# First chunk's turned blocks in the transform's input tiles, u turned ahead of them, next z loaded a chunk earlier, and a new instruction order

## The chip, the core and the metric

The kernel runs on one core of a Trainium2 chip. The metric is the device time of one execution in microseconds (us), lower is better. The engines are TensorE (PE, matmuls; PEld is its weight load), VectorE (DVE), ScalarE (ACT), GpSimd (POOL) and SyncE (SP, which here only issues DMAs). Each engine runs its own instructions strictly in the order in which they were written; they meet through semaphores.

## The reference

Eight batches of a gated attention unit, followed by a long-convolution block. All of it is one launch.

```python
# u, v: (8, 3136, 256)   z: (8, 3136, 64)
attn = maximum((z @ z.T) / S, 0) ** 2          # S = 3136, per batch
x    = u * (attn @ v)                          # (8, 3136, 256)
x1, x2, x3 = split(x @ w_proj, 3)              # 256 -> 3 x 256
conv = irfft(rfft(x2, axis=seq) * rfft(filter, axis=seq))
out  = (x1 * conv * x3) @ w_out
```

## The kernel before

**Tiling.** The sequence of 3136 is cut into 25 row tiles of 128 and, as columns, into seven chunks of 512, 512, 512, 512, 512, 256 and 320. Work goes batch by batch and chunk by chunk. For a chunk, a *unit* is a pair of row tiles: PE multiplies z with z into a PSUM pair `ps_s` (score, two 64-row matmuls side by side in the array), ACT or DVE applies the relu into an f32 tile `R_t` (L1899 on ACT, L1901 on DVE), ACT or DVE squares it into a bf16 tile `A_t` (L1908, L1910), and PE weighs v with it into two PSUM accumulators `ps_o` (L556, or L1701 when the rows are split in two halves). When all units of a chunk are weighed, DVE multiplies by u, which lies transposed in `uT_t`, and writes `xT_t` (L1954). The projection, the gates and a DFT of the middle part follow; after the seventh chunk of a batch its spectrum is multiplied by the filter's (`xh`) and transformed back, and `yT_t`, the output matmul and the store end the batch. This transform runs beside the next batch's chunks.

**Symmetry.** The score matrix is symmetric. Where a unit's row tiles belong to one of the next two chunks (REACH = 2), its squared tile is also turned by a DMA transpose from SP (function `mirror`, L1829) into a tile M1 or M2 (`M_t`, `M2e_t`, `M2o_t`), and the later chunk weighs that instead of computing it again. The squared tile must stay until the turn has landed. Squared tiles come from a pool of eight, used in a ring (`A_p`). In the first chunk of the first batch four of thirteen units are turned: two into M1 for chunk 1, two into M2e for chunk 2.

**Loads.** u is loaded and cast to bf16 by POOL's DMA into `un_t` (L630) and turned by SP into `uT_t` (`load_uT`, L1513). v is loaded by POOL (L649). The next batch's z comes in four pieces of 8, 8, 6 and 3 row tiles (`casts_at`): POOL loads a piece into `zn_t` (L630), DVE doubles it into `zd_t` (L1550), SP turns it into `zT_t` (L1557). Each chunk's loads are released on POOL by a copy of one element of the chunk's `xT_t` (`tick`, L639). The four pieces are released by the chunks 1 to 4 of the batch before.

**Order.** Nothing is scheduled at run time. A planner in the kernel's Python walks all tasks with a table of costs and writes the instructions out. The kinds of PE's tasks follow a fixed string ORDER, one letter a task: S score, W weigh, w and v the two halves of a row-split weighing, Q the spectrum's matmuls on quarters of the array, A, B and Z other matmuls. A second string, ENGINES, says for each task that ACT or DVE could do which of them does it. The order on DVE, ACT, SP and POOL comes out of the planner's own estimate of when a task is ready: for a DMA this is the end of its issue, its share of a common bus (`plan.bus`), a fixed time and an extra `late=` given with the task. These numbers decide only the order; at run time each instruction waits on semaphores.

```python
if task.moves:
    self.bus = max(end + DMA_GO[engine], self.bus) + task.moves
    lat = self.bus + DMA_DONE + task.late - end
```

Other pools that the change touches are `conv_in` (`c_p`, two tiles of 128 x 1024) and `spec_in` (`l_p`, two of 128 x 2048). They hold the inputs of the transform, which first needs them after the first chunks of the first batch.

Of the kernel before, what the change touches and what calls it, by code (L numbers as in the profile page):

```python
# [41 lines left out]


ORDER = (
    "ASBSWASWSWASWwSASvWSwSSWvwSSvSWSwSvSWWWWSSWWWWSSWWWWWSwSvSAWSAAAWAWAWWWBWSSWWAWWSAWWBSSAWWBSSwSvwSvA"
    "AwSWSvSWWWBBWWWABWAWSSAWBWAAWAWSSWSAWWBWWWWWSWSSWWBWSSSWWWWBWWAAWASwSAABWWWSSSvWWASSWAWWWWAAWWBAWAAA"
    "WAWSwSSvWWSSSWWWAAWWBAWASSWAABWAWWAWBwSSwSWAvSSvSWWWWWAWWSSWAAWWAWWSSWSSSWWAWSwSvQQwWSSWAAWvSQSWWAAW"
    "WSQAAWWAAWWQwwASSvSwwSAWAAWQvSSAWSvQvSWWWSQSWWWAAWWWAWSwSSWAWAvQwSwQvSwvSSvSWWAAWWAAWWWSQQWWWAAWSSSW"
    "WWAWQwQQvwQSSvAWASAWWWWAAWWASSWAWAAWWQSSWSSAWWSQQWAWWQSSWAWWAQQWWWWQSAWWAWWAWWSwSAvwSQvSWAWWASSWWAWW"
    "SSSWWWASSWAAWwSSvwSWWSwvSvSWWWWSSWWWWAWAWBABWSwSvSSWBWSSwSvWABWBWASSBWWAWBWBWSAWWAABWSSAAWAAWAWAWBAA"  # L50
    "SAWBASSWSSWBBAWWSSAWBWWBBBWWWWABWSSSWWSSAWAWWSQSWQAWAWWSSAWWWBAWBAWWWBQSAWWQwSwwSSWAAAWBWBAQvQvvSSQW"
    "BWSQQWWWBAWAWBAWWABWQSAWWASQWQSAWSSwwSvSvSWWWAAWWSQQWWWWWAASWWAWWSSAWQSSWWAAWAWQSWWAWSSWWAWWwSSvSWWS"
    "SSWWAWAWSSWAWWWWSSAWAWBWWASSWBWBBWSSSWWAABWSSSWWABWABWWSSSWWAWBBWAWAWWBASSWSSWAAAWBWSABWBBSwSvSWASWW"
    "BWBAWSWWABWWWSSSWwSSvAWBBWAAAWSSABWAAWBQQWAAWSSQWWWAWABWWQWSSWAWWQQSWBWWSSQWBWQSSWAAAWWAWWBWWSQSWWAA"
    "WWSSQWWSQSWWWQSQWAWAWSSWWAWWWWAABWAQSWAWWWABwSSAWAWWSQSvWWQSSWWAAWWASAWSSAWWSSSWWWSSSWWAWWAWAWWWWSSS"
    "WWWBBWAWSSSwwwSSvSvWWBvSSBBWBWAWWAAASWBBWBWAAWWBWASSAAWWBBSSWWWSSABWBSSwWASvSBWABWBBWSAWWBWWWBASSWAA"
    "SSAWABWSSWAAWABSQWAAWBBWQSSWWAWWSSQWWAAWWSQAWWWAWWWQQSWWWQSSWWBWQSSWAAAWWWSSQWWAWAWQSWAAWWASQWSQwSWA"
    "WAWAASSvBAWSWAWWBWWQQSWWWWWAAWSSQWWAAWAWWSQSWWAWAWWWSSSWAAWAWSSSwwwSvSvWWWSSvAAWWAWWWWSSSWWWBBBWBSSA"
    "WBABWSSSWBABSWABWSSWAWBAWWBSBWAAAWSSWWWBWBSSWAWASSWBBAWWSwSSvSWAWWBWWSSSWWWBAWWAWBAWSSBWWAAAWWSSQWAB"
    "AWWWSQSWWAAWAWAWBWAWSSAWAWSSSWWAASwQvSQWWSQSWWWAAAWSABBWWAWWQQSWWWSQwQWvSSWBWAAAWWSSSWWWWAQQWWWSQQWW"  # L60
    "WBAWAWSQBWAWSQSWWAAAWWASSWWWSSQWWWAWWSSWWSwSSvSwWWWWASvSAWWWAWAAWWSSAAWWSSWBWSSSWBWABAWSSSWABWBABWWW"
    "ASSWABWAABWWABWAWSSSWWBAWSSSWWBBWBABWBAWSSAABWBBWWAAWWWSSSWWBWBWSSWAAWSSAAWSSwQwSWAAWWBBQSvSvSWWWWAB"
    "WAWSQQWWAWABWQQSWWBWWSSSWAWWWQSSWWAAAWWWSSSWWAAASQAAWWQSAWAAWSQQWAAAWWQSQWWWAWWBWWSQSWWWWAWAQSwWWQvS"
    "SWAAAWSWWWSAWWSSAAAWWWwSSvSWAASSWWSSSWWWABWWWBSSBWWAWBBSBAWWBWAWBWSSSWWBSSWWABSSWBABWWWSSSWWWWBBWWBW"
    "WSSSWBAWwSSAAWBWBASAWWSvSSWWWASSWAWBBWWWZAAWWSSSWWABBWSQSWWWQSSWBBWWWWQQSWWWWAAWWAQSWAWSQQWWSSSWWWSS"
    "QWWWWBWBWWSQSWAAWWSSWWQSQWWWQSSWWWQSQWWWBWAWAWBAWWSSWAWAWSSAAWWQSSWWAWWAWWWQSZWWWSSSWWAWSSSWWWAWWWWW"
    "WWZZAAZBAAZZBBZZBBZBBZZZBZZQQZQZQZBQZQQQBZBQQQQZQQQQBZZZZZZZBZZZZBZZZZBBZZZBBBBBBBBBBBBBBBBBBBBBBBBB"
    "BBB"
)
# [357 lines left out]
def kernel(  # L427
# [1374 lines left out]
    def mirror(un, q_):  # L1802
# [12 lines left out]
                runs.append((a, i, [t]))  # L1815
        for a, i, ts in runs:
            made = mirror_tasks.setdefault((b, c, a), [])
            rows = N1 if ts[-1] == NT - 1 else P

            def go(a=a, i=i, ts=ts, rows=rows):  # L1820
                if (b, c, a) not in mirrors:
                    mirrors[b, c, a] = m_pool(c, a).tile()
# [6 lines left out]
                nc.sync.dma_start_transpose(out=o, in_=live[un][:rows, ds(i * cw, len(ts) * cw)])  # L1829
# [218 lines left out]
```

## Time and profile before

| | us |
|---|---|
| median of 3 runs (lowest, highest) | 977.6 (975.66, 978.12) |
| the profiled execution | 977.31 |
| its span, first to last instruction | 975.5 |
| PE busy | 950.4 (97%) |
| DVE busy | 870.8 (89%) |
| ACT busy | 836.0 (86%) |
| POOL busy | 197.4 (20%) |

Matmuls are pipelined, so that their durations overlap: what one costs is the distance from start to start. The end of the bracket in a row of the time line is how long the engine was idle before the instruction, and on what. A row of SP gives the time that the queue spent on issuing, not the landing; the landing is seen where somebody waited for it.

### The profile page before, as it was taken

Reading aid. Unit: us, or ns where it says so; the run is one execution under the profiler, and the core shown is the slowest. Engines: PE = TensorE matmul, PEld = TensorE weight load, DVE = VectorE, ACT = ScalarE, POOL = GpSimd, SP = SyncE. Lnnn points to the kernel's source line nnn. Section 1 sums busy time; section 2 is a strip of 40 time slices with the busy share of each in tenths; the row PEclk is TensorE's granted clock in tenths of the full one; section 3 lists DMA queues with packets and bytes.
Section 4 is the critical chain, followed back from the end, with each engine's and each line's share of the span. In section 5 each row is a group of like instructions: output and inputs, shape, how many; then the busy total and the mean of one; then the engine's idle time right before and its main releaser. Section 6 shows DMA issues by size and latency. Waiting matters only on the chain.

```text
span 975.5 us, 20058 instructions
## 1 busy us (share of the span) xinstructions
PE 950.4 (97%) x7097; PEld 469.8 (48%) x7097; DVE 870.8 (89%) x1508; ACT 836.0 (86%) x1145; POOL 197.4 (20%) x426
## 2 busy tenths in 40 slices
PE   6899999999999999999999999999999999999996
PEld 2344644445444554445544465444554455444654
DVE  7897998999889888899988999899899988889896
ACT  7686799999889998988898989799978899899783
POOL 5133311132012211213111131113201311000031
PEclk9999999999999999999999999999999999999998
DMA  9989889979799998988899999997999979786668
GB/s 151 148 161 171 135 171 165 172 142 167 168 199 202 135 177 188 199 172 134 178 200 192 169 154 179 216 184 143 152 201 210 187 139 182 179 190 142 179 195 259
DMA packets 332406, 170.36 MB, mean 175 GB/s; under 512 B 242598, under 2 KB 307942, under 8 KB 332304
## 3 DMA queue, kind: packets, MB, share of 16 engines
q1 hardware_dynamic: 302496, 132.43, 64.4%
q0 software_dynamic: 29168, 35.13, 24.5%
q10 hardware_dynamic: 640, 1.51, 0.5%
q8 instruction: 56, 0.92, 0.4%
q14 instruction: 46, 0.38, 0.1%
HBM read 90.26 MB, written 53.35 MB: 147 GB/s over the span
## 4 chain that ended last, share of the span: by engine, by line
PE 85%; DVE 6%; DMA 5%; issue 1%; ACT 1%; SPq 1%; POOL 0%; ACTq 0%; DVEq 0%; POOLq 0%
PE ps_o_t L556 45%; PE ps_s L556 35%; PE ps_o_t L1701 5%; DMA zn_t<-in_z_dram 1%; DVE A_t L1910 1%; DMA conv_in_t<-spec 1%; DVE R_t L1901 1%; DMA gs_t<-spec 1%; DMA spec_in_t<-spec 1%; DVE yT_t L1401 1%; DVE xh L1304 0%; DVE xT_t L1954 0%; DMA uT_t<-un_t 0%; DVE gate_t L1212 0%; DMA spec<-s_t 0%
## 5 line engine op out<-in xcount | busy, mean ns | idle before, releaser
L556 PE MATMUL ps_o_t<-A_t,v_t 128*128 128x512 bf16 (+2 forms) x1832 | 420.6, 356 | 3.8 <-DVE xT_t L1954 1.9
L1899 ACT ACTIVATE R_t<-ps_s 128x1024 f32<-128x1024 f32 (+2 forms) x351 | 328.3, 967 | 56.7 <-PE ps_s L556 51.8
L556 PEld LDWEIGHTS <-v_t 128*128 128x128 bf16 x2462 | 221.7, 98 | 231.6 <-issue 68.6
L1908 ACT ACTIVATE A_t<-R_t 128x1024 bf16<-128x1024 f32 (+3 forms) x310 | 301.8, 991 | 17.7 <-DVE R_t L1901 12.8
L1910 DVE TENSOR_TENSOR A_t<-R_t 128x1024 bf16<-128x1024 f32 (+3 forms) x186 | 207.5, 1128 | 10.1 <-ACT R_t L1899 7.1
L1901 DVE TENSOR_SCALAR R_t<-ps_s 128x1024 f32<-128x1024 f32 (+3 forms) x161 | 176.9, 1108 | 22.9 <-PE ps_s L556 17.4
L556 PE MATMUL ps_s<-zT_t 64*128 64x512 bf16 (+5 forms) x1355 | 165.0, 356 | 2.9 <-DVE R_t L1901 1.4
L639 POOL COPY tick<-xT_t 1x1 bf16<-1x1 bf16 x54 | 10.6, 196 | 692.0 <-DVE xT_t L1954 673.5
L556 PE MATMUL ps_s<-xT_t,wp 128*128 128x512 bf16 (+2 forms) x422 | 110.4, 353 | 0.3 <-DVE R_t L1901 0.3
L556 PEld LDWEIGHTS <-zT_t 64*128 64x128 bf16 (+1 forms) x1388 | 51.6, 99 | 90.8 <-issue 70.6
L589 ACT ACTIVATE x_t<-ps_s 128x512 bf16<-128x512 f32 (+2 forms) x133 | 72.8, 567 | 19.9 <-PE ps_s L556 16.8
L1954 DVE SCALAR_TENSOR_TENSOR xT_t<-ps_o_t,uT_t 128x256 bf16<-128x256 f32 (+2 forms) x224 | 75.9, 381 | 13.4 <-PE ps_o_t L556 8.2
L1304 DVE TENSOR_TENSOR xh<-xh,H 128x1024 bf16<-128x1024 bf16 x120 | 82.1, 685 | 2.9 <-ACT xh L589 1.1
L1212 DVE TENSOR_TENSOR gate_t<-ps_s,x_t 128x256 bf16<-128x256 f32 (+2 forms) x210 | 71.3, 383 | 9.3 <-PE ps_s L556 4.8
L556 PE MATMUL ps_o_t<-M_t,v_t 128*128 128x512 bf16 (+2 forms) x320 | 73.5, 353 | 0.0
L1401 DVE TENSOR_TENSOR yT_t<-ps_s,gate_t 128x512 bf16<-128x512 f32 (+2 forms) x96 | 58.3, 620 | 5.5 <-PE ps_s L556 4.6
L630 POOL DMA_DIRECT2D un_t<-in_u_dram x112 | 59.9, 556 | 7.4 <-issue 6.6
L649 POOL DMA_DIRECT2D v_t<-in_v_dram x112 | 59.6, 557 | 5.4 <-issue 3.5
L556 PEld LDWEIGHTS <-wp 128*128 128x128 bf16 x448 | 40.9, 98 | 39.7 <-issue 10.2
L556 PE MATMUL ps_s<-wp,xT_t 128*128 128x256 bf16 x398 | 58.6, 273 | 0.0
L1701 PE MATMUL ps_o_t<-A_t,v_t 64*64 64x512 bf16 (+4 forms) x562 | 56.7, 350 | 0.0
L556 PE MATMUL ps_s<-wo,yT_t 128*128 128x256 bf16 (+1 forms) x360 | 54.8, 273 | 1.1 <-DVE yT_t L1401 0.8
(170 smaller groups left out, 984.5 us busy)
## 6 DMA issues: line engine op xcount, KB each, us to landing
out_dram<-ost_t SPq DMA_DIRECT2D x60, 256.0 KB
spec<-s_t SPq DMA_DIRECT2D x96, 128.0 KB
spec_in_t<-spec SPq DMA_DIRECT2D x56, 192.0 KB
spec<-gs_t SPq DMA_DIRECT2D x56, 192.0 KB
v_t<-in_v_dram POOLq DMA_DIRECT2D x80, 128.0 KB, 4.6
un_t<-in_u_dram POOLq DMA_DIRECT2D x80, 128.0 KB, 5.5
conv_in_t<-spec SPq DMA_DIRECT2D x34, 256.0 KB
out_dram<-ost_t SPq DMA_DIRECT2D x18, 128.0 KB
```

Of the source, the lines that this page charges most:

```text
L556: wrote(nc.tensor.matmul(o, *args, **kw), o)
L589: got = nc.scalar.activation(out_, in_, AF.Copy)
L630: nc.gpsimd.dma_start(out=t[ds(j * N1, N1), lo - t0 : hi - t0, :], in_=x[:, n2 : n2 + hi - lo, :])
L1212: got = nc.vector.tensor_tensor(g[:, ::-1] if h == 0 else g, p, x, ALU.mult)
L1304: nc.vector.tensor_tensor(x[:, 1 - i], x[:, 0], h, ALU.mult)
L1401: got = nc.vector.tensor_tensor(yb["y"][:, dh, 0:w], p, gates[b, c, dh][:, 0:w], ALU.mult)
L1701: row_sums[dh] = h, nc.tensor.matmul(*args, **kw)
L1899: has_read(nc.scalar.activation(r, p, AF.Relu), p)
L1901: has_read(nc.vector.tensor_single_scalar(r, p, 0.0, ALU.max), p)
L1908: nc.scalar.activation(a, r, AF.Square)
L1910: (nc.vector if e == "DVE" else nc.gpsimd).tensor_tensor(a, r, r, ALU.mult)
L1954: nc.vector.scalar_tensor_tensor(x, f, inv_s2, ut, ALU.mult, ALU.mult)
```

## The change

The four turned units of the first chunk get their squared tiles from `conv_in` and `spec_in` in turn (`sends`), not from the ring. Of the first chunk's turns, the third and the fourth are issued only after u's first transpose has been issued. The pieces of the next z are released by chunks 0 to 3 from the second batch on; in the first batch they stay with chunks 1 to 4. The planner's numbers change: z's landing is put 2.5 us later, that of some loads at the end 1.2 us later, the first chunk's turns 2 us earlier, the bus counts as taken until 22 us, and PE's tasks that start before 14.3 us count double. ORDER and ENGINES are replaced whole; both keep their length, and ORDER keeps the number of each letter.

```diff
+LATE_Z = 4.0
+SLOW_TO = 14.3
 ORDER = (
-    "ASBSWASWSWASWwSASvWSwSSWvwSSvSWSwSvSWWWWSSWWWWSSWWWWWSwSvSAWSAAAWAWAWWWBWSSWWAWWSAWWBSSAWWBSSwSvwSvA"
+    "ASSABWSSSWAASWWSSWwwwSSvwvSvSvSSWWSWWWSSWWWSSWWAWAWWwSSSwWAvSSvSWAWWWWWWBBWWBSSWWWAWWASwwSwSSvWAAAWS"
...
 ENGINES = (
...
         cost = task.cost[engine]
+        if engine == "PE" and start < SLOW_TO:
+            cost *= 2
...
-        return on("SP", go, 0.55, deps, [home.slots], moves=0.235 * nt, late=0.5), box
+        return on("SP", go, 0.55, deps, [home.slots], moves=0.235 * nt, late=1.7), box
...
+    plan.bus = 22.0
...
+    lent = {}
+
+    def sends(un):
+
+        b, c, k = un
+        if b or c or not any(c < home[t] <= c + REACH for t in plans[b, c][k][1]):
+            return 0, None
+        i = lent.setdefault(un, len(lent))
+        return i, (c_p, l_p)[i % 2] if i < 4 else None
...
-        i = c - 1
+        i = c - (b == 0)
         if n < B and 0 <= i < 4:
             t0, t1 = ((0, 8), (8, 16), (16, 22), (22, NT))[i]
...
-                a = on("POOL", cast, 1.1, [tick_], [zn_p.slots], moves=0.09 * (t1 - t0), late=LATE_CAST)
+                a = on("POOL", cast, 1.1, [tick_], [zn_p.slots], moves=0.09 * (t1 - t0), late=LATE_Z)
...
+            first_u = [(u_tasks[0, 0], ISSUED)] if b == c == 0 and sends(un)[0] >= 2 else []
...
-                "SP", go, 1.3, [q_, *((d, ISSUED) for d in made[-1:])],
-                [] if made else [m_pool(c, a).slots], moves=0.78 * len(ts) * cw / 512, late=LATE_TURN + 2.0 * (b == c == 0),
+                "SP", go, 1.3, [q_, *((d, ISSUED) for d in made[-1:]), *first_u],
+                [] if made else [m_pool(c, a).slots], moves=0.78 * len(ts) * cw / 512, late=LATE_TURN,
...
-            a_p = As_p if n > len(pair) else A_p
+            a_p = As_p if n > len(pair) else sends(un)[1] or A_p
...
-                A = a_p.tile()
+                A = a_p.tile([P, 2048 if a_p is l_p else 1024])
```

More of the change, by code (lines that the diff above doesn't have):

```diff
@@ L50 @@
[L50 to L54, printed above, removed]
@@ new lines @@
+    "WWWSSwAWAWWASSvWAWWSSWABAWWWWSSwSWAWBSwSSvWAASWSvSWAWWAWSWAWAWWSSAWWAWSSSWAWWSwQvwSSvQWSQSWAAAWWAWWA"
+    "WSSAWWWASQWAWAwwSvQwSvSAAwvSQSWAAWWAWSQSvWAAWWWAWWSQSWWAAWwSSSWWAwSSwwQQSvvvSvSWAAAWWAWWWWQQSWWAWWSQ"
+    "SwwAAWWSSSvvSQWAAWWQQWWWWQSWWAAWAAWAWWSQSWWSQSWAWASSWWQSQWAWWQSAWWWAWSSAWWWAAWWAWSSwwQvSWWQvSSWWWAWW"
+    "WSSAWWAASwSwSwSSvvSWWAWAWSvSSWWAAWWWAWWBWBWSSAWAWSSwwSSvWBWSvSSWAWWWBBAWWBWAWSSWWBBWBWBWASSWAAWSSBBW"
+    "AWSSSWABWBWAWBWASSWBBWAWWBSSAAWWWBASSWBAWSSSWAAWAAWAASSWAWWQSWWWWBQQAWWAWABWBWASwSWBAwQSwSvvQvSQBWAB"
@@ new lines @@
+    "AWSQAWQQWAWWWWSSSWWBAAWQQSWWWAWAwSSWSQvwSWWSSQvWWWAWAAWAWWQQSWWWWWSSSWAAWWSQAAAWWWSSSWWAWWSSWAWWSSSW"
+    "WASSWWWSSwSvWWWAWAWAWAWWBSSWAAWBWWBWSSSWBWSSSWWABWBWWAWSSBAWWBWWSSBWBWSSWAAWAASSWABAWABWBASSwSWAWBWA"
+    "BSvBBWAWWWWSSAWWSSBWWSSSWWAAWQSAWAQSAWWAWWQSABWWAWWQSSWWBBWWQQSWWWABWQSQWAAWAWQSSWWWWWSSAWWAWBQSABWW"
+    "SQSWAWWSSWWQSSWWAQSWWWWAAAWAWAAWQSWWAAWAWWSSwSWBWAWvSQWABAWSQAAWWWSSSWWASSAWWAAAWSSSWWSSSWWWWWAWWWWS"
+    "SBWWAWWBSwSWBBWASwSSvwvSSAAWBABWBAWWBASvSWABWBWWABWASWBAAWWSSBBWBAAWSSSWABAWBSwSSvSWAWSWWBWBWAWBWBWW"
@@ new lines @@
+    "SSAAWBWSAWAAAWSSQWSSSWWWWQSQWAWAWBWWSQQWWABAWWWAWSSBWAWSSQWBWSSWWWQSQWWAWAWWQSSWWWWAWQSSwQWAWSQvSWAA"
+    "WWSSABWWSQAABWWWWQSQWWWWAAWAWAWSSAAWWSQSWWWWSSSWWWAAWAWAAwSSwSWAAAWSwSSvvvSWAWWWWAWWWSSSWWWABWSSBWAB"
+    "WASSBAWAWBWBSSAWWWBWASSBWWWAABWWBSSWWABAWWSSwSWSSvSWWBWBWSSWAABWAWBWWBBWASSWWWWSSWBBWAASSAAWSQSWWBWS"
+    "SSWWAWWWBAWAWSSAWBWBWAAWQwSQAAWAWWQvSSSWWQQSWBWWWWWSSWAWBWAAWSQWBwQQSWWWSSSWWSQvSWQSWWAWAAWWWSQAWWAA"
+    "WAAAWWWSQAWWQSAWAAWWSQSWWWAAWWWSQSWWWSwSSwSvvSSWWWWAAAWBSSWWWAAWSSWAWAWWASSWWSSSWBAWSSWABWBABSSWWAAW"
@@ new lines @@
+    "AABWBWBWAWBSSBWBAWWASSBAWWASSBWAWSSAWBBWSSAWAAWBBAWWBWBSSWWWWSSWWWABBWAAWSSSWSwwQSWAWWBWBSvvQQSWWWBA"
+    "WSSWWAWWQQSWWABWSSQWWBAAWSSSWAAWWWSSAWAWWAWQSAWAWQSQWWAAWASQAWWQQWAAAWSQWWWWSSQWWWWSQSWWWAAWWAWQSSWA"
+    "WSSWWAWAAWBWASSWAWAAWWSSwSWWASvSSWWASSWWWWSSWWAWBWWBWBWBWSSWBABWBSSWAASSBBWBAWBAWSSSWWBWBWWSSSWWWWAW"
+    "WASSBWAAWSSwSWBBAWWAWBBWSvSSWBBWWWWSSAWWABWSSABWWQQSWWWSSSWWWWSQSWWWAWWAWQQSWWAAWAWSSQWWQSSWWWSSSWWW"
+    "WSSQWWWWQQAWBWAWWSQSWWQSSWBAWBWWSQSWWAWWBWWAABWWSSWBAWWSSQWWWWAQSAWWAWWAWWQSSWWWWSSSWWSSWWWWZAWWZWWW"
@@ L68 @@
+    "WAZZAZABAAZZBZBZBBZZBZZBZBQZQQZZZQBZQQBZQQQQQZBQQQQQBZZZZZZBZBZZZZZZBZZZBZZBBBBBBBBBBBBBBBBBBBBBBBBB"
     "BBB"
@@ L87 @@
-    "daaaadadddddaaddadaaaaaaaaaddadaaaaaaaadadaadaadadadaadaddadaadaaaaadaaaaddaadaaaadadddadaaadadadada"
-    "aaddaddddaadaaadaaaaaadaaaaadaadddaaaaaadaaaaaaaaaadddaaaaaadaaaddaadaaaaaaadaaddaadadadaaaaadadaaad"
-    "aaaaaaaadaaadaaaaaaaaaaaddaaaadaaaadaadddaaaaa"
+    "adaddddddaadadaadaaadaaaaadadaaadadadaadaaaddaadaddadadaaadddadaaadaddddaaadaddadadadaaaadddadadadaa"
+    "daadaadadaddaadaaaaaaaadaaaaaaaaddaaadaadaaadddaaaaaaaaaddaaddaaddaadaaaaaadadaaddddaadaaaaddadaddaa"
+    "daaaadddadaaaaaaaaadaadaddaaaadaddaaddadddadddadaaaadadaddadaadaaadaaaddddaaaaddaaaddaadadaaddaaaaaa"
@@ new lines @@
+    "dddaadddadadadaaaadaadaaddaaaaddadaadadaaaaadaaadaaadaaaaddaaaaaaadaddaaaadaaaadaaaaaaadaaaadddaaada"
+    "aaaadaaadddaaadaaadddadaaddaadadaadaddaadaddddaadddaaaadaaaddadaaadddaaadaaadaaaadaaddadaaaddaaaddaa"
+    "adadaaaaadaddaaaadddaaaaaaaaadaaddaaaadadaaaaaadaaaadaaadaaaaddaaaadaaaaaaaaaadaaaaaadaaaaadaadadada"
+    "aaaaddaaadaaddaaadaadaaaadadadadaddddaaaaaaadaaadaaaaadaadaaaaadaaaaaaaaadadaaaaaddaaadaaadaaddaddad"
+    "aadaaadaaaaddaaaaaaadddaadaaaadaaaaadddaadaadaadddaadaaaadaaaaddaaaadaddaaaaaaaaaadaaddaaaaaadaaddda"
@@ new lines @@
+    "aaadddaddaaaaaadaaddadaddadadadaaddaaaaaaddadaaddaaaaaaaaaaaaaaaaadaaaadaaadaaaaaddadaadadaadddaadaa"
+    "adaddaaaadaaaadddaaddddadadaaaaadadadaaddaaaddaaaadadaaaaddadaaaddaaaaaddadaaddaadaadaaaadaaaaadadad"
+    "daadadaaaaadaaaaaaaaaadddadaaadadaaaddadadaadaaadadaddddaaddaddaaaaadaaadaadadddaadaaaaddaadadadadaa"
+    "adaaaaadaaadaaddaaaadaaadadaddaaadadaaadaaaaadadddaadadaadaaddaaaddaaadaaddadaaaaaaaaaadaaaddaadaaad"
+    "aaddaaadaaaaaaaaaaadddaaaaddaddaadadaaaaaddaaaaaaaaaaaaadaddaaaddaaaaaaadddaaaadaddaaaddaaaddddaaaaa"
@@ L90 @@
+    "dddaadaaaadddaaaddadadadaaaadddaadadaaaddaaadaaadddaaaaaaaaaaadddaaddddadaddaaaadaaaadaaaadadaaaddaa"
+    "addaaaadaaaadaaadddaaaaadadaaaaaaaaadaaaaaaaddaadaaaaaadaaaaaddaaadaaadadaddaaddddadaddaddaddaaadada"
+    "addaaaaddaadddadaadaaaaaaaddaaadaadaaaaaadddaaaaddadadaadadaadaaadaadadaaaaddaaaaddaaaaaaddadaaaadaa"
+    "aaddaadaaaddaaaadaaddaadddaaaaaaaadaadaaaaaaaadaaaaaadaddaaaaaddadadaadaadaddaadaadddadaaaaaaaddaaad"
+    "aaaaaaaadaaadaaaaaaaaaaaddaaaadaaaaadadadaaaaa"
 )
```

33 lines of the change are left out of this document (1 added, 32 removed).

## The prediction

> **What bounds the kernel now.** I read the page's first lines, then the busy time by stretches, then what TensorE (PE) waited for, then the chain, and last the time line of the stretches where PE was idle. The profiled execution took 977.31 us with a span of 975.5, so 1.8 us lie around the span; the median of the three runs is 977.6. The sum below is made against 977.31, and 0.3% of it (2.9 us) is about what a measurement of this kernel can tell from no change.
>
> Busy time by stretches (length; PE, PEld, DVE, ACT, POOL with instruction counts; clock, DMA share, GB/s):
>
> ```profile
> span 975.5 us, 20058 instructions
> ```
> ```profile
> 0.00:25.00 25.00, 17.18 (x104) 6.50 (x106) 18.98 (x53) 17.96 (x24) 13.42 (x35) 1.00 1.05 150
> 25.00:35.00 10.00, 6.36 (x35) 1.91 (x32) 5.49 (x9) 6.92 (x8) 0.18 (x1) 1.00 0.95 129
> 35.00:60.00 25.00, 24.49 (x137) 9.76 (x137) 24.75 (x43) 19.52 (x24) 7.34 (x14) 1.00 0.85 149
> 60.00:300.00 240.00, 240.00 (x1814) 115.61 (x1813) 214.90 (x361) 207.48 (x277) 54.03 (x113) 1.00 0.92 168
> 300.00:325.00 25.00, 23.91 (x196) 10.51 (x195) 21.67 (x40) 22.24 (x34) 3.81 (x8) 1.00 1.04 176
> 325.00:500.00 175.00, 175.00 (x1286) 88.94 (x1285) 158.92 (x264) 156.39 (x213) 34.06 (x74) 1.00 0.90 172
> 500.00:525.00 25.00, 24.55 (x167) 11.70 (x165) 21.32 (x38) 21.75 (x30) 3.80 (x8) 1.00 0.99 211
> 525.00:905.00 380.00, 379.89 (x2787) 187.38 (x2786) 349.06 (x595) 338.41 (x460) 68.51 (x150) 1.00 0.89 175
> 905.00:950.00 45.00, 42.98 (x442) 26.36 (x440) 39.17 (x73) 36.17 (x67) 8.17 (x16) 1.00 0.70 190
> 950.00:975.60 25.60, 16.07 (x147) 11.15 (x144) 16.54 (x39) 9.12 (x17) 4.04 (x8) 0.90 0.82 258
> ```
>
> PE is never idle in 240 of 240 and 175 of 175 us, and for 0.11 us in 380. In those 795 us only a shorter PE stream can gain anything. The idle time that a better order could take stands in few places: 7.8 us up to 25, 3.6 in 25 to 35, 0.5 in 35 to 60, 1.1 in 300 to 325, 0.45 in 500 to 525, 2.0 in 905 to 950, 9.5 at the end. PE's longest waits by cause (total, times, longest):
>
> ```profile
> PE ps_s L559 <- ACT xT_t L589: 4.8, 1, 4.8
> ...
> PE ps_s L559 <- ACT T L870: 1.6, 1, 1.6
> PE ps_s L556 <- DMA conv_in_t<-spec: 1.3, 1, 1.3
> PE ps_s L556 <- DVE zT_t L593: 1.3, 2, 0.8
> ```
>
> The 4.8 is the arrival of the first z, which the change leaves alone.
>
> **Term 1, PE's stream.** In the chain of waits:
>
> ```profile
> 75.48 0.32 PE ps_s L556
> 75.81 1.73 PE ps_o_t L556 x8
> 77.53 0.22 PE ps_s L556
> 77.75 3.45 PE ps_o_t L556 x16
> ```
>
> Sixteen matmuls of 512 columns take 3.45 us, 0.216 each. The piece at 77.53 follows matmuls of its own kind and takes 0.22; the piece at 75.48 follows matmuls on 64 rows and takes 0.32. A change between half-array and whole-array matmuls so costs 0.10 us. The built programs have 544 such changes in PE's order before and 520 after: 24 x 0.10 = 2.4 us less. The new order also has 7159 matmuls instead of 7097: 62 more, since more score blocks go as quarters of the array beside row-split weighings. Packed four to a slot of 0.216 they cost nothing, unpacked 62/4 x 0.216 = 3.3 us. Laying both streams end to end on the four quarters at that spacing gives 0.9 more for the new one, which I take. Term 1: **-1.5** (-2.4 to +0.9).
>
> **Term 2, the first chunk's turned blocks and u.** Four of the first chunk's thirteen squared tiles are turned by DMA for later chunks. Until a turn has landed, its tile is not free, and in the old kernel those are four of the ring of eight A tiles.
>
> ```profile
> 27.60 0.59 PE L556 MATMUL ps_o_t<-A_t,v_t 128*128 128x512 bf16 x2 [0.97 <-ACT A_t L1908]
> 28.82 1.02 PE L556 MATMUL ps_o_t<-A_t,v_t 128*128 128x512 bf16 x4 [0.63 <-DVE A_t L1910]
> ...
> 33.24 0.59 PE L556 MATMUL ps_o_t<-A_t,v_t 128*128 128x512 bf16 x2 [1.89 <-DVE xT_t L1954]
> ```
> ```profile
> 26.49 1.06 ACT L1908 ACTIVATE A_t<-R_t 128x1024 bf16<-128x1024 f32 x1 [1.03 <-DMA M_t<-A_t]
> ...
> 31.46 1.06 ACT L1908 ACTIVATE A_t<-R_t 128x1024 bf16<-128x1024 f32 x1 [1.58 <-DMA M2e_t<-A_t]
> ```
> ```profile
> 27.55 1.22 DVE L1910 TENSOR_TENSOR A_t<-R_t 128x1024 bf16<-128x1024 f32 x1 [2.07 <-ACT A_t L1908]
> ...
> 32.34 0.76 DVE L1954 SCALAR_TENSOR_TENSOR xT_t<-ps_o_t,uT_t 128x256 bf16<-128x256 f32 x2 [2.44 <-DMA uT_t<-un_t]
> ```
> ```profile
> 14.69 4.25 SPq L1829 DMA_TRANSPOSE M_t<-A_t  x2
> 19.04 8.59 SPq L1829 DMA_TRANSPOSE M2e_t<-A_t  x2
> 27.73 3.61 SPq L1513 DMA_TRANSPOSE uT_t<-un_t  x2
> ```
>
> The two squares at 26.49 and 27.55 could have run from 25.46 and 25.48 (their starts less the idle before them); they waited for turned blocks, and so PE idled 0.97 and 0.63. With those four tiles in conv_in and spec_in, which nobody else uses yet, both waits go. Then PE waited 1.89 for xT, and xT for u, which SP issued only behind four blocks. The three waits are 3.49 us; without any, PE stands at its first weighing of chunk 1 at 29.75.
>
> What is late next is u itself, for it now stands third instead of fifth. The first turn had landed by 26.4, u by 32.3: four steps of 1.47 us. Third place is then 29.35, xT starts at about 29.4, and PE follows as before, 0.90 behind xT (33.24 less 32.34), at 30.3. That is 2.94 us earlier. Of it 0.36 belongs to term 1, as PE's stream up to this weighing is 17.62 us long in the new order and 17.98 in the old. Ends: if third place takes as long as the M2e pair's last block did (31.4), PE comes at 32.35 and the term is -0.5; if nothing else binds, the three waits go whole, with up to 0.5 us of half-hidden delay: -4.0. Holding the third and fourth turns behind u costs nothing: their block M2e is read in chunk 2, which PE reaches some 15 us later. Term 2: **-2.6** (-4.0 to -0.5).
>
> **Term 3, the first 15 us.** PE runs at half speed here, whatever the clock column says:
>
> ```profile
> 12.27 1.03 PE L556 MATMUL ps_o_t<-A_t,v_t 128*128 128x512 bf16 x2
> ...
> 15.57 0.60 PE L556 MATMUL ps_o_t<-A_t,v_t 128*128 128x512 bf16 x2
> ```
>
> The new order puts a second score pair and the second transpose group in front of the transpose that waited 1.6 us for the DFT table (T). The wait as such goes. But the chain to the third score pair is z's cast, its transposes and DVE's copy into zT, and DVE now has one relu and one square of 1.2 us among them, and the first zT copy has moved to ACT. I count **-0.4**; -1.6 if the whole wait on T is won, +1.2 if one DVE operation stands ahead of the zT copy.
>
> **Term 4, next z a chunk earlier from the second batch on.** Each piece is three DMAs on POOL, a doubling copy on DVE and a turn on SP.
>
> ```profile
> 319.47 0.36 DVE L1550 COPY zd_t<-zn_t 128x768 bf16<-128x768 bf16 x1 [2.04 <-DMA zn_t<-in_z_dram]
> ```
> ```profile
> 301.25 1.25 SPq L1557 DMA_TRANSPOSE zT_t<-zd_t  x1
> 302.60 1.94 SPq L1031 DMA_DIRECT2D spec_in_t<-spec  x3
> ```
>
> DVE, strictly in order, stood 2.04 us before this copy with relu and squares behind it, and PE, whose scores need those tiles, lost 1.1 us in this stretch; the same thing cost 0.45 in 500 to 525. The new due time puts the copy 2.5 us further back in DVE's order, and the load moves out of a stretch with a DMA share of 1.04. Behind POOL's moved DMAs are only v and u loads, needed a chunk or more later. Term 4: **-1.5** (-1.5 to 0).
>
> **Term 5, the end.** PE idles 2.0 us in 905 to 950, of which 1.3 is one wait for a conv_in load; loads into other tiles get a later due time there, which only changes the order. **-0.4** (-2.0 to +2.0). **Term 6:** the order is written anew everywhere, and some place will wait that did not. Nearest row: the old order's 795 quiet us hold 0.11 us of PE idle, and its two flaws 1.5. **+0.6** (0 to +4).
>
> Sum: -1.5 -2.6 -0.4 -1.5 -0.4 +0.6 = -5.8, so 977.3 - 5.8 = **971.5 us**. All terms at their low ends, with term 1 at -1.5, give 966.7.
>
> **Rivals.** *u comes no sooner and PE cools.* The third place lands at 31.4, PE idles from 29.75 to 32.35, 2.6 us, and falls back to half speed. The rows of term 3 show half speed at 12.27 and full speed at 15.57: up to 3.3 us of steady work at half speed lose up to 1.6. Term 2 becomes -0.5 + 1.6 = +1.1 and the time 975.2, within 0.3%. For it: SP's 8.59 us for the M2e pair shows the queue standing full until 27.6. Against it: u follows the fourth block by only 0.9 us, and after the 1.89 us gap at 33.24 the next pair took 0.59, so a gap of that length does not cool PE. A rule for this stands in the Trainium skill, "TensorE: Matmul & The Clock Gate", section "Why this matters for your kernels": gaps of PE over about 3 us bring the half clock back. By that rule this rival's gap falls just short and the time would be 973.6; no row here has a gap long enough to test it.
>
> *Slower: the earlier z stands in the way of the transform.* In chunks 0 to 3 of batches 1 to 6 the turned z takes 1.25 us of SP each, directly ahead of spectrum loads of the batch before. If two pieces a batch delay those loads in full, that is 12 x 1.25 = 15 us and term 4 is lost: 977.3 - 4.3 + 15 = 988; it is slower (over 980.2) from 7.2 us exposed. Against it: at 301.25 a z turn already stands right before such a load, and from 60 to 300 PE was never idle.
>
> *The new order gives its gain back.* DVE is busy 24.75 of 25 us in 35 to 60, so a PE that comes 3 us earlier may wait there. Were term 2 lost to it and term 6 at +2, the time is 977.3 - 1.5 - 0.4 - 1.5 - 0.4 + 2 = 975.5. Against it: DVE too saves its 2.07 and most of its 2.44 idle.
>
> **Chances.** Forecast, with variants better than it, 0.78; PE cools or the gain given back, both within 0.3%, 0.13 together; the z rival, or a sum of new waits that turns it slower, 0.09. The range from 966.7 to 976.0 takes in the low ends and both cases within 0.3%.
>
> **What would show it.** Right: in the changed profile no ACT or DVE wait on M_t or M2e before 30 us; u issued third by SP; PE's first weighing of chunk 1 near 30.3 with one wait on xT before it; no DVE wait before a zd_t copy; PE idle below 0.5 us between 35 and 905. Wrong: that weighing after 32; pairs of 512-column matmuls at 1.03 instead of 0.60 after 20 us; PE waits on spec_in_t or DVE's xh in chunks 0 to 3; more than 3 us of PE idle between 35 and 905.

## The result and the profile after

The changed kernel takes 972.71 us in the median of seven runs (969.16 to 975.71) against 978.81 us before (975.66 to 982.41): a ratio of 0.9939, 95% interval 0.9912 to 0.9965. Twelve later runs against 23 gave 973.05 us against 978.68 and a ratio of 0.996 (0.9936 to 0.9985). The forecast was 971.5 us, 5.8 under the profiled execution before; the medians differ by 6.1 and 5.6.

The profiled execution of the changed kernel, though, took 975.71 us with a span of 973.9, only 1.6 less than before. It is the slowest of its seven, and its profile says why. Busy time by stretches, the same stretches and columns as in the prediction (length; PE, PEld, DVE, ACT, POOL; clock, DMA share, GB/s):

```profile
0.00:25.00 25.00, 15.78 (x103) 6.66 (x104) 20.70 (x55) 15.72 (x22) 13.31 (x35) 1.00 1.03 137
25.00:35.00 10.00, 6.95 (x33) 2.32 (x31) 6.80 (x9) 6.55 (x7) 0.82 (x2) 0.92 1.21 160
35.00:60.00 25.00, 24.91 (x141) 9.90 (x138) 23.10 (x38) 17.43 (x20) 6.84 (x14) 0.96 0.81 148
...
300.00:325.00 25.00, 25.00 (x211) 10.70 (x202) 23.13 (x43) 24.31 (x35) 3.80 (x8) 1.00 0.89 179
...
500.00:525.00 25.00, 25.00 (x169) 11.58 (x167) 23.57 (x39) 19.91 (x27) 3.80 (x8) 1.00 1.05 206
525.00:905.00 380.00, 379.93 (x2804) 188.75 (x2802) 346.39 (x584) 341.15 (x467) 67.24 (x147) 1.00 0.86 174
905.00:950.00 45.00, 43.32 (x434) 26.76 (x432) 41.21 (x81) 34.60 (x65) 9.70 (x19) 0.96 0.68 191
```

The two flaws in the middle are gone: PE is busy 25.00 of 25.00 in 300 to 325 (23.91 before) and in 500 to 525 (24.55). But up to 35 us nothing was won: PE idles 9.2 and 3.1 us there, against 7.8 and 3.6 before, and the clock shows 0.92 and 0.96 behind it. The time line of PE and DVE at that place:

```profile
29.91 0.61 PE L560 MATMUL ps_s<-zT_t 64*128 64x512 bf16 x4
33.57 1.01 PE L560 MATMUL ps_o_t<-A_t,v_t 128*128 128x512 bf16 x2 [3.06 <-DVE xT_t L1971]
34.38 1.06 PE L560 MATMUL ps_o_t<-M_t,v_t 128*128 128x512 bf16 x2
```
```profile
32.67 1.42 DVE L1971 SCALAR_TENSOR_TENSOR xT_t<-ps_o_t,uT_t 128x256 bf16<-128x256 f32 x4 [3.04 <-DMA uT_t<-un_t]
```

PE was through with chunk 0 earlier than before and then stood 3.06 us for u, which landed at 32.6; the pairs behind take 1.01 and 1.06 instead of 0.59. That is the rival "u comes no sooner and PE cools", in one execution, and two of the prediction's signs of being wrong showed in it: the weighing after 32 us, and pairs at half speed after 20 us. A second profile of the same kernel (*again*, 970.68 us, span 968.9) shows the other case:

```profile
28.16 0.60 PE L560 MATMUL ps_s<-zT_t 64*128 64x512 bf16 x4
28.70 0.60 PE L560 MATMUL ps_o_t<-A_t,v_t 128*128 128x512 bf16 x2
```
```profile
27.79 1.41 DVE L1971 SCALAR_TENSOR_TENSOR xT_t<-ps_o_t,uT_t 128x256 bf16<-128x256 f32 x4
```

No wait, full clock, and chunk 1 weighed from 28.70. The issues on SP of the two executions, first the late one, then *again*:

```profile
17.27 3.95 SPq L1846 DMA_TRANSPOSE M_t<-spec_in_t  x1
21.33 6.97 SPq L1519 DMA_TRANSPOSE uT_t<-un_t  x1
28.39 1.44 SPq L1846 DMA_TRANSPOSE M2e_t<-conv_in_t  x1
```
```profile
15.91 4.73 SPq L1846 DMA_TRANSPOSE M_t<-spec_in_t  x1
20.75 1.41 SPq L1519 DMA_TRANSPOSE uT_t<-un_t  x1
22.25 1.37 SPq L1846 DMA_TRANSPOSE M2e_t<-conv_in_t  x1
```

In both u is issued third, as planned. In one the issue took 1.41 us, in the other 6.97.

The end shows how little else separates the two. The 224 multiplications by u (`xT_t`) serve as marks in DVE's time line; in the tables and text below, "first mark" is the start of the first of them. The last group, in *before*, the first profile after, and *again*:

```profile
922.26 0.55 DVE L1954 SCALAR_TENSOR_TENSOR xT_t<-ps_o_t,uT_t 128x192 bf16<-128x192 f32 x2 [0.26 <-PE ps_o_t L556]
```
```profile
919.96 0.95 DVE L1971 SCALAR_TENSOR_TENSOR xT_t<-ps_o_t,uT_t 128x192 bf16<-128x192 f32 x4
```
```profile
914.58 0.95 DVE L1971 SCALAR_TENSOR_TENSOR xT_t<-ps_o_t,uT_t 128x192 bf16<-128x192 f32 x4
```

Between the two profiles after, the first mark differs by 4.88 us and the last group by 5.38. Mark by mark the gap opens to 6.5 by the second chunk, 1.6 of it the half clock, stays to 0.1 us for whole batches, and falls by 0.5 and 0.4 behind places where ACT in *again* waits for turned blocks (1.87 us before 187.88, 0.90 before 765.09) and the late execution does not. So an execution can be cut in three: up to the first mark, from the first to the very last mark (the middle), and from there to the end of the span (the tail).

| profile | first mark | middle | tail | span |
|---|---|---|---|---|
| before | 32.34 | 890.2 | 53.0 | 975.5 |
| before_again (below) | 29.41 | 889.8 | 57.4 | 976.5 |
| after | 32.67 | 888.0 (1.6 of it half clock) | 53.3 | 973.9 |
| again | 27.79 | 887.5 | 53.7 | 968.9 |

### The profile page after: what moved, and what is told of

Same layout as the page of the kernel before. It is cut to its first block, busy times and chain, and to the rows that moved or that the text cites. A ratio compares the mean times of both kernels' runs of the same rounds, so it can differ in the third digit from the quotient of the medians.

```text
span 973.9 us, 20208 instructions
## 1 busy us (share of the span) xinstructions
PE 951.2 (98%) x7159; PEld 474.1 (49%) x7159; DVE 862.6 (89%) x1500; ACT 840.0 (86%) x1153; POOL 197.3 (20%) x426
## 5 line engine op out<-in xcount | busy, mean ns | idle before, releaser
L1916 ACT ACTIVATE R_t<-ps_s 128x1024 f32<-128x1024 f32 (+4 forms) x341 | 318.3, 962 | 55.4 <-PE ps_s L560 51.7
L1925 ACT ACTIVATE A_t<-R_t 128x1024 bf16<-128x1024 f32 (+3 forms) x322 | 311.9, 995 | 7.0 <-DVE R_t L1918 5.2
L1918 DVE TENSOR_SCALAR R_t<-ps_s 128x1024 f32<-128x1024 f32 (+4 forms) x171 | 189.9, 1122 | 23.5 <-PE ps_s L560 12.3
L1927 DVE TENSOR_TENSOR A_t<-R_t 128x1024 bf16<-128x1024 f32 (+2 forms) x170 | 188.9, 1122 | 7.3 <-ACT R_t L1916 6.5
L593 ACT ACTIVATE x_t<-ps_s 128x512 bf16<-128x512 f32 (+2 forms) x136 | 76.1, 579 | 19.7 <-PE ps_s L560 16.1
L560 PE MATMUL ps_o_t<-M_t,v_t 128*128 128x512 bf16 (+2 forms) x312 | 71.3, 352 | 0.0
L597 DVE CAST x_t<-ps_s 128x512 bf16<-128x512 f32 (+2 forms) x75 | 46.0, 623 | 9.4 <-PE ps_s L560 5.1
```

The lines of the kernel that those rows point to most:

```text
L560: wrote(nc.tensor.matmul(o, *args, **kw), o)
L593: got = nc.scalar.activation(out_, in_, AF.Copy)
L1916: has_read(nc.scalar.activation(r, p, AF.Relu), p)
L1925: nc.scalar.activation(a, r, AF.Square)
L1927: (nc.vector if e == "DVE" else nc.gpsimd).tensor_tensor(a, r, r, ALU.mult)
```

## The experiments

PE's busy share in the later profiles is not comparable with that of the first two: some matmul records are missing, which shows as 26 to 33 holes of 0.2 us. They are compared by the marks and by single rows.

### The two kernels once more

*again* has no edit.

> The changed kernel unaltered, for a second profile beside the variants below. Theory S (the start counts: u's landing sets when PE reaches chunk 1, and it varies): PE's first weighing of chunk 1 lies near 30.3 us where u lands near 29.4, the half clock after 33.4 us is then absent, and the whole execution is 2 to 4 us shorter than the first profiled one (975.7). Theory R (the gain lies in PE's stream and in the next z, the start gives nothing): the weighing is again near 33.6 us and the median is still 5 to 7 us under the kernel before.

Theory S came out in kind: the weighing at 28.70, no half clock before 934 us, the span 5.0 us shorter, which is more than the 2 to 4 expected. R's median (5.6 under before) came out as well, so the start is not the whole gain.

*before_again* is the kernel before, unaltered.

> The kernel before, unaltered, for a second profile of its start. If u's landing varies between executions of one kernel as it did between the two of the changed kernel (27.8 against 32.7 us), xT of chunk 0 starts more than 1 us away from the 32.34 of the first profile and the later chunks are displaced by as much; the waits on the next z near 300 and 500 us (1.1 and 0.5 us) come again, since they lie in the order of DVE and not in the start.

```profile
29.41 0.76 DVE L1954 SCALAR_TENSOR_TENSOR xT_t<-ps_o_t,uT_t 128x256 bf16<-128x256 f32 x2 [1.62 <-PE ps_o_t L556]
```

The first mark lies at 29.41, not at 32.34, and it waits for PE, not for u. In this execution neither ACT nor DVE waited for a turned block at all. So the three waits of 3.49 us on which term 2 was sized belonged to one execution, not to the kernel. The whole took 978.3 us nonetheless, since the tail is 4.4 us longer:

```profile
PE ps_s L556 <- DMA spec_in_t<-spec: 2.0, 1, 2.0
...
PE ps_s L556 <- DMA A_t<-spec: 1.5, 3, 1.0
```

The last transform's loads came late and PE's clock was halved once at 933 us. The waits on the next z came again (DVE 2.15 us before the copy at 316.65).

### The start: lent tiles and u's place

*start_as_before* takes out both the lent tiles and u's place ahead of the third and fourth turn, *lent_only* takes out u's place, *u_third_no_lent* the lent tiles.

```diff
-        return i, (c_p, l_p)[i % 2] if i < 4 else None
+        return i, None
...
-            first_u = [(u_tasks[0, 0], ISSUED)] if b == c == 0 and sends(un)[0] >= 2 else []
+            first_u = [(u_tasks[0, 0], ISSUED)] if False else []
```

> The changed kernel with the first chunk's turned blocks again in the ring of A tiles and u's turn no longer ordered ahead of the third and fourth block (it comes fourth); the strings and the next z stay new. Theory S: 2.6 us slower than the changed kernel (0.5 to 4), ACT and DVE wait for M_t and M2e before 30 us. Theory R: within 0.5 us of the changed kernel, and PE's first weighing of chunk 1 again near 33 us.

> The changed kernel with the lent tiles but without the order of u's turn ahead of the third and fourth block (u comes fourth). The variant without both was 1.9 us slower than the changed kernel in the mean. If the lent tiles carry that, this is within 0.7 us of the changed kernel when u lands as early; if u's place carries it, u lands one turn later (1.4 us) and this is 1.5 us slower. PE has no wait on an A tile before 30 us in either case.

> The changed kernel with u's turn ahead of the third and fourth block, but the blocks in the ring of A tiles. With the two variants run already it makes the four cases of lent tiles and u's place: with neither 1.9 and with the lent tiles alone 2.2 us slower than the changed kernel in the mean. If u's place alone carries the start, this is within 0.7 us of the changed kernel; if the two are needed together, ACT or DVE waits for M2e's turn, now behind u, PE stands 2 us or more before 30 us, and this is 2 us slower or more.

| | median, us | ratio to before (95%) | first mark |
|---|---|---|---|
| both (again) | 973.05 | 0.996 (0.9936 to 0.9985) | 27.79 |
| neither (start_as_before) | 975.93 | 0.9961 (0.9938 to 0.9983) | 30.61 |
| lent tiles alone | 975.06 | 0.9972 (0.9951 to 0.9993) | 30.19 |
| u third alone | 982.83 | 1.0049 (1.0022 to 1.0077) | 27.41 |

Without both, ACT waits for the turns again and PE with it; with the lent tiles alone PE waits for xT, at half clock afterwards:

```profile
28.01 1.02 PE L560 MATMUL ps_o_t<-A_t,v_t 128*128 128x512 bf16 x4 [2.50 <-ACT A_t L1925]
```
```profile
31.09 1.01 PE L560 MATMUL ps_o_t<-A_t,v_t 128*128 128x512 bf16 x2 [2.32 <-DVE xT_t L1971]
31.89 1.06 PE L560 MATMUL ps_o_t<-M_t,v_t 128*128 128x512 bf16 x2
```

Against *again* these two are 2.8 and 2.4 us late at the first mark and 1.5 and 4.4 at the last. In these single profiles each half moves the wait to the other place. By runs the two edits together are worth 1.9 us in the means (19 runs after, 973.2, against 975.0), but the ratios to before, 0.996 and 0.9961, are alike: an effect is not shown. The case of u alone answered another question than it was put: its first mark is the earliest of all and no turn is waited for, but its marks then lose 2.9 us up to the second chunk at 44 us, 1.3 near 80, 1.5 near 557 and some 3.8 between 750 and 792, and end 7.6 us behind *again*.

None of the three moves its instructions alone. The planner wrote the order anew, so that ACT's instructions stand in another order than in the changed kernel in 18 and 19 places in the first two and in 45 in the third, some of them hundreds of microseconds from the start. The first marks are those of single executions, too, and the load described next took 10.0 and 9.9 us in the first two against 7.5 in *again*. What each edit is worth by itself stays open.

### Why u comes late: the load of wp

POOL issues the load of the projection's weights (wp, 384 KB, cast on the way) right behind u's. In the profile before it took 11.7 us to land (the last number of its row among the DMA issues), through the very time in which SP's turns are issued:

```profile
wp<-in_moe_w_proj_dram POOLq DMA_DIRECT2D x1, 384.0 KB, 11.7
```

The same row in the first profile after, and in *again*:

```profile
wp<-in_moe_w_proj_dram POOLq DMA_DIRECT2D x1, 384.0 KB, 12.3
```
```profile
wp<-in_moe_w_proj_dram POOLq DMA_DIRECT2D x1, 384.0 KB, 7.5
```

The two go together. In the kernel before the load took 11.7 us where the first mark lies at 32.34, and 8.1 and 8.0 us where it lies at 29.41 and 29.76 (*before_again*, and *before_copy_later* below, whose start is unaltered); in the changed kernel it took 12.3 us with the mark at 32.67, and 7.5 and 7.7 us with 27.79 and 27.93 (*again*, and *z_later_only* below, with the same start). POOL issued it at 16.24 us in the first profile after and at 13.93 in *again*, so it landed at about 28.5 and 21.4; the long issue on SP, u's in the one (to 28.30) and the second block's in the other (to 20.64), ends 0.2 to 0.8 us before that. Such a match does not say which of the two holds up the other. The next two runs do.

*wp_behind_u* lets POOL wait for u first:

```diff
-    nc.gpsimd.dma_start(out=wp16[:], in_=moe_w_proj.rearrange("(t p) n -> p t n", p=P))
...
+    def load_wp():
+        nc.gpsimd.tensor_copy(tick[:], uT[0, 0][0:1, 0, 0, 0:1])
+        nc.gpsimd.dma_start(out=wp16[:], in_=moe_w_proj.rearrange("(t p) n -> p t n", p=P))
+
+    on("POOL", load_wp, 0.8, [u_tasks[0, 0]])
```

> The changed kernel with the load of the projection's weights (wp) issued by POOL only when chunk 0's turned u has landed, instead of right behind the loads of u. Theory W (that load takes the DMA engines from the turned blocks and u, which then crawl): SP issues the first three turns without a hold over 3 us, xT of chunk 0 starts at or before 27.8 us in this execution and the others, the runs' upper end falls, and the median is 1 to 3 us below the changed kernel's 973. Rival V (u comes late because the loads of v and u ahead of it are late): u lands anywhere from 27 to 33 as before, no gain. Third possibility: wp lands after 31 us and the first projection waits for it on PE, 1 to 3 us slower.

Median 970.18 us (969.66 to 973.02), ratio 0.9921 (0.9892 to 0.9949). Theory W holds nearly as put: u's issue takes 1.25 us, the first mark is at 27.99 (27.8 was the limit), and one issue still takes 3.32 (3 was the limit). Of the third possibility the wait came, but not the loss: the first projection waits 1.21 us for wp. The orders of DVE, ACT and SP are those of the changed kernel, instruction by instruction, and on POOL only the load of wp has moved, here and in the next run.

```profile
27.99 1.41 DVE L1976 SCALAR_TENSOR_TENSOR xT_t<-ps_o_t,uT_t 128x256 bf16<-128x256 f32 x4
```
```profile
16.54 3.32 SPq L1851 DMA_TRANSPOSE M_t<-spec_in_t  x1
19.97 1.25 SPq L1518 DMA_TRANSPOSE uT_t<-un_t  x1
```
```profile
31.15 0.60 PE L560 MATMUL ps_s<-xT_t,wp 128*128 128x512 bf16 x2 [1.21 <-DMA wp<-in_moe_w_proj_dram]
```

*wp_behind_block* puts the load one turn earlier: POOL's copy reads the second turned block in `M_t` instead of `uT_t`.

```diff
+            if (b, c, a) == (0, 0, 1) and len(made) == 2:
+                on("POOL", lambda at=j_: load_wp(at), 0.8, [t_])
...
+        nc.gpsimd.tensor_copy(tick[:], mirrors[0, 0, 1][0:1, at : at + 1])
```

> As the variant with wp behind u, but POOL issues the load of wp one turn earlier, when chunk 0's second turned block has landed. Theory W: its data starts to flow only as u has landed, xT of chunk 0 starts near 28 us as there, wp lands 1.4 to 2 us earlier and PE's wait of 1.2 us for it goes: 1 us below that variant, near 969. Rival: the load takes the DMA engines from u's turn again, xT starts after 29 us and nothing is gained on that variant.

Median 969.5 us (968.13 to 971.1), ratio 0.9905 (0.9873 to 0.9937), the fastest of all. The wait for wp is gone and u is nearly as early:

```profile
19.12 1.25 SPq L1518 DMA_TRANSPOSE uT_t<-un_t  x1
```
```profile
28.24 1.40 DVE L1977 SCALAR_TENSOR_TENSOR xT_t<-ps_o_t,uT_t 128x256 bf16<-128x256 f32 x4
```
```profile
29.14 0.61 PE L560 MATMUL ps_o_t<-A_t,v_t 128*128 128x512 bf16 x2
29.59 0.59 PE L560 MATMUL ps_o_t<-M_t,v_t 128*128 128x512 bf16 x2
30.02 0.59 PE L560 MATMUL ps_s<-xT_t,wp 128*128 128x512 bf16 x2
```

The gain lies in the distribution of the runs and not in the best of them: the profiled execution (971.10 us, first mark at 28.24) is no faster than *again* (970.68, 27.79). The twelve runs with wp moved lie between 968.1 and 973.0 us, the 19 of the changed kernel between 969.2 and 977.4. They belong to different comparisons, though, and the intervals of the ratios to before, here and for the changed kernel, partly overlap. That the late executions are missing because u is no longer late is the likely reason, and it is not shown for the runs without a profile. Their clocks do not tell it: the first profile after, with u late, has a granted clock of 0.994, but so have the profiles of *wp_behind_u* and *z_later_only* (below), whose u was early; they lost theirs to 6.83 us of half clock from 935 and 936 us on, in the tail.

*before_wp* makes the same edit in the kernel before.

> The kernel before with one edit: the load of wp is issued when chunk 0's second turned block has landed. Theory W (wp's load is what makes the turned blocks crawl and hold the A tiles): the waits of ACT and DVE on M_t and M2e shrink below 0.5 us each, xT of chunk 0 starts at 28.5 to 29.5 us instead of 32.3 or 29.4, and the kernel before gains 1 to 3 us (ratio 0.997 to 0.999). Rival: four tiles held by turns are too few for the ring in any case; xT stays after 30 us, within 0.5 us of the kernel before.

Median 977.5 us (972.94 to 984.0), ratio 0.9991 (0.9964 to 1.0018): not told apart from before, and the forecast gain of 1 to 3 us did not show. The first mark is at 28.77 and no turn is waited for, as W says:

```profile
28.77 0.74 DVE L1960 SCALAR_TENSOR_TENSOR xT_t<-ps_o_t,uT_t 128x256 bf16<-128x256 f32 x2
```

But in the other profiles of the kernel before without that wait it lies at 29.41 and 29.76, so only 0.6 to 1 us is left to win there, and the runs still spread over 11 us. The tail is one source of that spread (53.0 to 57.4 us in the profiles of this kernel); whether there are others is not shown.

### The next z

*before_copy_later* and *z_later_only* keep every other instruction in its place and move the next z's alone: in the kernel before the copy and the turn go 2.5 us back, and in the changed kernel load, copy and turn go back to about where they were. They do it by writing those tasks out later than planned:

```diff
+            self.held.append((start + hold, task.no, task, engine))
...
+                if 0 < b < B - 2:
+                    d.hold = t.hold = 2.5            # before_copy_later
+                if b in (1, 2, 3, 4):
+                    a.hold, d.hold, t.hold = 17.0, 14.5, 17.0    # z_later_only
```

> The kernel before with every instruction in its place but the copy and the turn of the next z, which come 2.5 us later on DVE and SP in batches 1 to 5. The forecast's term 4: DVE's waits of about 2 us before these copies go, PE's 1.1 us near 300 and 0.5 near 500 with them, 1.5 us faster than the kernel before. Rival: PE gets them back elsewhere, within 0.5 us of the kernel before.

> The changed kernel with every instruction of PE and ACT and every other one in its place; only the next z's load, copy and turn come 17, 14.5 and 17 us later on POOL, DVE and SP in batches 1 to 4 (the copy 2.5 us closer behind its load, as before the change). The forecast's term 4: DVE waits up to 2 us before some copies again, PE idles 1 to 1.5 us near 300 and 500 us, 1.5 us slower than the changed kernel. Rival A: PE's own lead hides these waits, under 0.5 us. Rival B: the 20 us by which the variant with z as before and the new order was slower come from the late z itself; then 8 us or more here.

Median 978.72 us for the first, ratio 1.0005 (0.9979 to 1.0031): nothing gained. Its stretches show the stalls gone (23.91 and 24.55 before; the rest to 25 is the holes of missing records):

```profile
300.00:325.00 25.00, 24.63 (x211) 11.04 (x203) 24.09 (x45) 23.50 (x36) 3.80 (x8) 1.00 0.93 177
...
500.00:525.00 25.00, 24.73 (x169) 11.73 (x171) 22.80 (x41) 22.06 (x31) 3.90 (x9) 1.00 1.00 217
```

Against *before* the marks gain 1.29 us at 326 and 0.66 at 524, and lose 0.2, 0.6 and 0.3 between 174 and 289 and 0.9 at 582: the copies, moved back, now meet others' work there. The second: median 972.74 us, ratio 0.9948 (0.9926 to 0.9971), not to be told from the changed kernel; its marks lose about 0.6 us against *again* in the batches that were altered, and 1.0 more near 784 in one that was not, where ACT waits for turned blocks. Rival A holds. So the stalls of 1.5 us stay away from the changed kernel even with z late, and z's place by itself is worth about 0.6 us by the marks of one execution. By elimination the new order is what keeps them away; no run shows that directly.

### One part with the strings of the whole

*strings_alone* is the kernel before with the new ORDER and ENGINES; *z_as_before* is the changed kernel with the old chunks and due time for z, left to the planner:

```diff
-        i = c - (b == 0)
+        i = c - 1
...
-                a = on("POOL", cast, 1.1, [tick_], [zn_p.slots], moves=0.09 * (t1 - t0), late=LATE_Z)
+                a = on("POOL", cast, 1.1, [tick_], [zn_p.slots], moves=0.09 * (t1 - t0), late=LATE_CAST)
```

> The kernel before with the new order of PE and the new choice of engines, and nothing else of the change: ring of eight A tiles, u behind three turned blocks, next z as before. Forecast's terms: 1, 3, 5 and 6 remain, -1.7 us against the kernel before, so 4 us slower than the changed kernel (ratio to before 0.998). Theory R: the order carries all but the z term, -4.5 us (0.9955). Third possibility: the order was made for the lent tiles and without them PE waits for A tiles in the first chunk, 0 or slower.

> The changed kernel with the next z's pieces in chunks 1 to 4 of every batch and the old due time of the cast. Both theories: 1.5 us slower than the changed kernel (ratio to before 0.995), with PE idle about 1 us again near 300 us and 0.5 near 500. Rival: the new order alone removed those waits; then no difference from the changed kernel and no idle time there.

Both were far off every expectation: 991.8 us (ratio 1.0138, 1.011 to 1.0166) and 992.62 us (1.0142, 1.0118 to 1.0165). The built streams have 7153 and 7159 matmuls, and 520 changes each, like the changed kernel's, so PE's work is not longer; its middle is 906.3 and 906.9 us instead of 887.5, lost in some thirty places by 0.2 to 1.6 us and in one by 6.3 and 5.4, where a transform waits for its input and the clock is halved after it:

```profile
639.18 0.40 PE L560 MATMUL ps_s<-spec_in_t,S 49*64 49x256 bf16 x2 [2.82 <-DMA spec_in_t<-spec]
```

Since *z_later_only* with a z about as late but every other instruction in its place loses nothing measurable, the 20 us do not come from z. What is left is what the planner makes of the strings: a letter names only a kind of task, and a different estimate of readiness puts other tasks and other DMAs behind the same letters. ACT, which handles no next z, has its instructions in another order in 58 places in *z_as_before* and in none in *z_later_only*. The strings fit the one plan for which they were found. These two runs therefore do not measure what they were meant to, the strings' own share.

## Why the prediction was right, point by point

**Term 1** (PE's stream, -1.5). The counts stand, but no run isolates it; *strings_alone* was to do so and failed. The middle as a whole, terms 1, 4 and 6, was forecast at -2.4 and measured 887.5 in *again* against 889.8 and 890.2, -2.3 to -2.7; the first profile after gives 888.0, or 886.4 without its half clock, -3.4 to -3.8. How the middle divides among the three terms stays open.

**Term 2** (-2.6) is the step that was mis-sized, and its argument was too narrow. It read one execution as the kernel: the A-tile waits were not there in the next profile, and its first mark lay at 29.41. It then counted steps of 1.47 us from a first landing at 26.4, and that start was the wrong one: wp's load ran until 26.5 us in that execution, and with the load moved (*before_wp*) nothing waits for a turn any more. The weighing expected at 30.3 came at 28.70 in one profile and at 33.57 in the other, never between. Where u came early, the first mark moved from 29.41 to 27.79, -1.6, where u came late from 32.34 to 32.67, +0.3, and the half clock behind it cost 1.6 more. This holds term 3 too, so the start was forecast at -3.0 and gave at best about half. The forecast took the 8.59 us of the M2e pair on SP, from 19.04 on, for a queue that stands full; it did not ask what filled it.

**Term 3** (-0.4). In the first profile after, z's second group landed late (DVE's cast at 10.02 had waited 1.21 us for it) and PE stood 3.3 us; in *again* 2.0. All PE's waits up to 15 us come to 7.7 us before, 9.2 in the first profile after and 7.9 in *again*: the wait on T went, as forecast, and one on z's cast took its place. No gain shows here.

**Term 4** (-1.5) came out in the profile, but not by the cause that was forecast: PE idles 0.00 in both stretches, and no wait stands before a copy of z there (in *again* one of 1.04 us, for an earlier turn of z). In place the two moves are worth about 0 in one kernel and 0.6 in the other.

**Term 5** (-0.4). Tails of the kernel before in its two unaltered profiles: 53.0 and 57.4; after: 53.3 and 53.7. Its waits on `A_t` loads do not appear after. The mean says -1.7, but two profiles of each cannot bound it: the changed kernel's variants with the same order at the end have tails of 53.2 to 55.4, those of the kernel before 53.7 and 57.0, which makes the difference about -1.0 in the mean of all.

**Term 6** (+0.6). In 35 to 905 PE idles 0.25 us with the first profile; in *again* two places cost the marks 0.5 and 0.4 us more. A cost of about 0.6 fits, though the gains of terms 1 and 4 cannot be told from it.

**The rivals.** "PE cools" did happen, in the profiled execution, with a gap of 3.06 us instead of 2.6 and at the price forecast: 1.6 us of the gap that opens up to the second chunk is half clock. The forecast gave it a part of 0.13 as a fate of the kernel; it is a fate of single executions, and how many of the 19 met it is not known. The z rival did not show: PE's waits on `spec_in_t` come to 0.6 us in all in *again*, both after 920 us. "Gain given back in 35 to 60" did not show.

So the middle came out as forecast as a whole, the start gave less, and the rest of the 5.6 to 6.1 us must lie in the tail or in how often u is late, neither of which two profiles can size. That the number is so close is partly luck.

## What to carry to other kernels

Before a wait of one execution is priced as the kernel's, see whether it is there in a second profile: here the start moved by 3 to 5 us between executions of one and the same program, more than the edit that was made to it. Ask of a transfer that crawls what else is in flight: in the changed kernel, moving one load that nobody yet needed behind the turns gained 2.5 to 3.5 us in the median, where lending tiles and u's place showed no gain clear of the noise. The same move gained nothing that could be told in the kernel before. An order found by search belongs to the plan it was found on, so a part of such a change is tested by moving its instructions alone, not by planning again.

## What the runs showed of the hardware

**The clock is granted in steps of 3.41 us.** In the nine profiles with more than one stretch of half clock these begin on one grid of 3.41 us, which lies elsewhere in each execution, and those that end inside the span last one or two steps (3.41 or 6.83 us). In the first profile after they begin at 33.44, 937.97 and 968.69 us: 265 and 9 steps apart. What a gap costs depends on how it lies in a step. Busy time of PE and the clock, per step: the first profile after (gap 3.06 us), *lent_only* (gap 2.32 us), *start_as_before* (gap 2.50 us):

```profile
30.02:33.44 3.42, 0.49 (x4) 0.00 (x0) 0.77 (x3) 1.56 (x2) 0.00 (x0) 1.00 1.24 171
33.44:36.85 3.41, 3.28 (x8) 1.20 (x9) 2.91 (x4) 0.52 (x2) 2.47 (x5) 0.50 0.78 126
```
```profile
27.70:31.11 3.41, 1.09 (x8) 0.20 (x7) 3.38 (x6) 3.03 (x4) 0.00 (x0) 1.00 0.89 192
31.11:34.53 3.42, 3.42 (x9) 1.22 (x10) 2.76 (x4) 0.60 (x1) 2.48 (x5) 0.50 0.33 27
```
```profile
23.62:27.03 3.41, 1.89 (x9) 0.60 (x8) 2.94 (x3) 1.70 (x3) 0.00 (x0) 1.00 1.19 167
27.03:30.45 3.42, 2.44 (x13) 0.88 (x13) 1.06 (x2) 2.13 (x3) 0.00 (x0) 1.00 1.25 178
30.45:33.86 3.41, 3.41 (x18) 1.25 (x17) 3.41 (x7) 3.38 (x5) 1.75 (x4) 1.00 0.32 59
```

The longer gap of the last, 2.50 us, fell across two steps and left the clock alone; the shorter one of 2.32 fell into a single step and halved the next. The Trainium skill, "TensorE: Matmul & The Clock Gate", section "What's actually happening", gives a free-running window of 3413 ns and says that the half clock comes after an idle window. The grid agrees; the window need not be idle, though, since 1.09 us of work in it did not help. The rule of gaps over 3 us that the prediction weighed, and by which a gap of 2.6 would have been harmless, is therefore no bound. At the end of the span steps with 2.55 to 3.0 us of busy PE were followed by half clock too; there many small matmuls run, and what is counted in them stays open.

**A casting load beside DMA transposes.** The issue of one and the same turn of u took 1.25 us in both runs with wp's load held back, and 1.41, 2.18 and 6.97 us in three executions with it in flight. Where wp's load ran beside the turns it took 7.5, 7.7 and 12.3 us itself, where it came behind the second block or u 6.8 and 6.5. How the two share the DMA engines stays open.
